# Value loads ahead of key loads in one DMA queue: an attention decode kernel that streams its cache

## The chip, the cores and the metric

The kernel runs on one core of a Trainium2 chip. The metric is device time in microseconds (us), median of several executions. All runs told of here are in the fast state. Ratios are taken against executions of the kernel before on the same chip in the same rounds. Engines are named as the profile names them: PE is TensorE (matmuls), DVE is VectorE, ACT is ScalarE, SP is SyncE, which issues nearly every load. A load is issued when SyncE hands it to the queue, and has landed when the last of its 16 semaphore events has come.

## The reference, cut to what matters

One decode step of a transformer block: 8 sequences, 32 heads, 4096 cached positions, head size 128, bf16. The parallel MLP is small.

```python
xn = layernorm(x)                                   # x: 8 x 1 x 640
q = (xn @ wq).reshape(8, 1, 32, 128).transpose(0, 2, 1, 3)
scores = einsum("bhqd,bhkd->bhqk", q, k_cache) * 128 ** -0.5
o = einsum("bhqk,bhkd->bhqd", softmax(scores), v_cache)
return x + o.reshape(8, 1, 4096) @ wo + mlp(xn)     # "@ wo" is the projection
```

The two caches are 268 MB each and every byte is used once, so the kernel is a stream of 4 MB loads with some work behind each.

## The kernel before

The caches are cut into T = 64 stretches `t`: four heads of one sequence, 4 MB of keys K(t) and 4 MB of values V(t). There are two buffers for keys and two for values. Three quarters of the key work is done on VectorE (multiply, add halves, reduce; two rounds each stretch), one quarter on TensorE (transposes and small matmuls). The softmax is done for two stretches at a time, a pair (t even, t+1). After it, PV(t), 32 matmuls of 128x512, uses V(t).

Every operation is added with a position `pos`; each engine runs its operations in the order of `pos`, and the scheduler derives the semaphore waits from the buffers named in `R` (read) and `W` (written).

```python
NK, NV, NS = 2, 2, 4                    # key buffers, value buffers
def ld(pos, dst, src, W, sem, R=()):
    add("sp", pos, lambda e: e.dma_start(dst, ...), R=R, W=W, sem=sem)
ld(-99.0, wq_sb, ...)                   # query weights, in the space of the value buffers
def pvpos(i):
    return 2.0 + i                      # PV(t) comes after the scores of t+2 on PE
for t in range(T):
    pos = (-100.0, -98.0)[t] if t < NK else t - 1.5
    ... ld(pos, K(t)) ...               # K(t+2) at t + 0.5: waits for the multiplies of t (DVE)
    pos = (0.45, 1.2)[t] if t < NV else t + 0.6
    ... ld(pos, V(t)) ...               # V(t) at t + 0.6: waits for PV(t-2) (PE)
                                        # the last V in three pieces: 64, 32, 32 columns
for hg in range(NG):
    ld(hg * B + 3.65, wo_sb, ...)       # projection weights, one load for 8 stretches
# scores of t on PE: t - 0.6 .. t - 0.1;  on DVE: t .. t + 0.13
# softmax of a pair (t, t+1): t + 1.28 .. ;  PV(t): t + 2.0 .. ;  its row sum on PE: t + 2.21
# projection on PE: 2 * pair + 5.33, behind the softmax's small matmuls of its position
```

## Time and profile before

| what | number |
|---|---|
| time, median of 3 | 1298.23 us (1298.19 to 1298.57) |
| span of the profiled run | 1296.1 us |
| read from HBM | 551.8 MB, mean 426 GB/s |
| busy: VectorE, TensorE, ScalarE | 87%, 50%, 39% |
| last value bytes landed (semaphore events of the trace) | 1290.9 us |

The page's 40 slices of the kernel before, share of the DMA engines in tenths and GB/s:

```profile
DMA  9989999999999999999999999999999999999997
GB/s 405 426 360 431 430 435 430 428 430 432 434 431 430 427 435 434 429 432 425 437 433 428 434 425 436 433 427 436 425 435 432 429 435 426 434 432 428 432 430 330
```

This is a kernel bound by its loads. Two slices fall out of line: the third (65 to 97 us) and the last.

Two stretches in the windows view of the kernel before, one around the third slice and one near the end. After the stretch and its length come the busy us of each engine with its number of instructions, the granted TensorE clock (1.00 is full), the DMA share and GB/s:

```profile
80.00:95.00 15.00, 9.48 (x112) 6.24 (x113) 14.89 (x7) 8.06 (x18) 0.00 (x0) 0.50 0.68 273
1283.00:1285.00 2.00, 1.73 (x20) 0.30 (x8) 0.00 (x0) 0.22 (x1) 0.00 (x0) 0.50 0.92 385
```

All 16 DMA engines together were silent for 2.5 us (85.74 to 88.27 in the packet records).

Issues of the loads, from the page (count, size, median us from issue to landing), and the chain of waits in its late, regular part (start, us, what):

```profile
KV_sb<-in_A_k_cache_dram SPq DMA_DIRECT2D x64, 4096.0 KB, 26.8
KV_sb<-in_A_v_cache_dram SPq DMA_DIRECT2D x63, 4096.0 KB, 35.2
```

```profile
1191.90 3.62 PE PV_ps L615 x24
1195.54 35.18 DMA KV_sb<-in_A_v_cache_dram
1230.76 3.61 PE PV_ps L615 x32
```

One value buffer is held 3.6 us by PV and in the queue for 35.2 us; with the gap, 38.86 us for a pair of stretches, 16.8 MB, 432 GB/s. A load takes 9.7 us of the queue, so a value load is asked for long before it is needed.

Who waited for whom (us in total, times, longest), engines first, then SyncE's queue:

```profile
PE PV_ps L615 <- DMA KV_sb<-in_A_v_cache_dram: 141.3, 56, 3.7
DVE Y_sb L543 <- DMA KV_sb<-in_A_k_cache_dram: 70.4, 34, 2.3
```

```profile
SPq L178 <- DVE Y_sb L543: 940.2, 56, 19.3
SPq L365 <- PE PV_ps L615: 53.7, 44, 17.8
```

SyncE waits for VectorE's multiply most of the time (940 of 1296 us), and the value load stands behind that wait in its program. Only V(3) to V(10) were issued clearly later than the end of PV(t-2), by 0.6 to 2.4 us. From V(11) on each followed PV(t-2) within about 0.2 us. K(61) and V(59) on SyncE show it, next to the chain above, where PV(57) ended at 1195.52:

```profile
1194.00 0.33 SPq L365 DMA_DIRECT2D KV_sb<-in_A_k_cache_dram  x1
1195.54 0.33 SPq L365 DMA_DIRECT2D KV_sb<-in_A_v_cache_dram  x1
```

The end, from the timeline (start, us, engine, line, operation): the last reduction on VectorE, PV(62), the three parts of PV(63), and the store of the output.

```profile
1275.31 3.35 DVE L550 TENSOR_REDUCE S_sb<-Y_sb 128x48 f32<-128x3072 bf16 x1
1281.14 3.59 PE L615 MATMUL PV_ps<-KV_sb,P_sb 128*16 128x512 bf16 x32 [1.07 <-DMA KV_sb<-in_A_v_cache_dram]
1286.03 1.04 PE L615 MATMUL PV_ps<-KV_sb,P_sb 128*16 128x512 bf16 x16
1288.51 0.80 PE L615 MATMUL PV_ps<-KV_sb,P_sb 128*16 128x512 bf16 x8 [1.45 <-DMA KV_sb<-in_A_v_cache_dram]
1290.96 1.06 PE L625 MATMUL PV_ps<-KV_sb,P_sb 128*4 128x128 bf16 x32 [0.68 <-DMA KV_sb<-in_A_v_cache_dram]
1294.36 0.35 SPq L775 DMA_DIRECT2D out_dram<-out_sb  x1
```

Each part of PV(63) starts when its piece lands, the last one 0.05 us after the last landing. 5.2 us of the span are left after it.

### The profile page before, as it was taken

The page shows a single profiled execution, that of the slowest core. Times are in us where ns is not written, and L with a number is a line of the kernel's source. Part 1 is how long each engine was busy: PE and PEld are TensorE (multiplying, and loading weights), DVE is VectorE, ACT ScalarE, POOL GpSimd, SP SyncE. Part 2 cuts the span into 40 slices and gives each one's busy share as a digit, 9 for nine tenths or more (in the row PEclk, how much of TensorE's full clock was granted, in tenths as well). Part 3 has the DMA queues.
Part 4 walks back from the last instruction along what each step waited for, and adds up shares of the span by engine and source line. Part 5 has one row for each costly group of instructions (what it writes and reads, how often), then busy time and mean ns, then how long its engine had stood idle before and what let it go on. Part 6 is the DMA issues. An engine that isn't in the chain of part 4 may idle for free.

```text
span 1296.1 us, 19692 instructions
## 1 busy us (share of the span) xinstructions
PE 650.0 (50%) x7853; PEld 408.1 (31%) x7853; DVE 1121.7 (87%) x586; ACT 500.3 (39%) x1241; POOL 0.2 (0%) x4
## 2 busy tenths in 40 slices
PE   2854554554454445454545544544544554445555
PEld 0432333333233233232333332332322332323332
DVE  3799999998898888988988988988888888889885
ACT  1543443344343243343343442443432443433442
POOL 0000000000000000000000000000000000000000
PEclk9655556555565555556555555555665556655566
DMA  9989999999999999999999999999999999999997
GB/s 405 426 360 431 430 435 430 428 430 432 434 431 430 427 435 434 429 432 425 437 433 428 434 425 436 433 427 436 425 435 432 429 435 426 434 432 428 432 430 330
DMA packets 23519, 551.99 MB, mean 426 GB/s; under 512 B 2297, under 2 KB 6481, under 8 KB 6482
## 3 DMA queue, kind: packets, MB, share of 16 engines
q1 hardware_dynamic: 23472, 551.80, 99.3%
q8 instruction: 7, 0.11, 0.0%
q14 instruction: 6, 0.05, 0.0%
q10 hardware_dynamic: 34, 0.02, 0.0%
HBM read 551.80 MB, written 0.01 MB: 426 GB/s over the span
## 4 chain that ended last, share of the span: by engine, by line
DMA 77%; DVE 10%; PE 9%; issue 3%; ACT 0%; SPq 0%; DVEq 0%
DMA KV_sb<-in_A_v_cache_dram 75%; PE PV_ps L615 7%; DVE Y_sb L543 5%; DVE Y_sb L547 3%; DVE S_sb L550 2%; DMA KV_sb<-in_A_wq_dram 2%; PE TR_ps L451 1%; PE CH_ps L564 0%; DVE M_sb L562 0%; SPq L365 0%; PE PV_ps L625 0%; PE PV_ps L689 0%; PE TR_ps L462 0%; DVE rinv_sb L596 0%; PE TR_ps L664 0%
## 5 line engine op out<-in xcount | busy, mean ns | idle before, releaser
L543 DVE TENSOR_TENSOR Y_sb<-KV_sb,qbc_sb 128x6144 bf16<-128x6144 bf16 x128 | 429.0, 3352 | 95.9 <-DMA KV_sb<-in_A_k_cache_dram 70.4
L550 DVE TENSOR_REDUCE S_sb<-Y_sb 128x48 f32<-128x3072 bf16 x128 | 429.2, 3353 | 4.4
L514 ACT ACTIVATE KT_sb<-TR_ps 128x1024 bf16<-128x1024 bf16 x256 | 254.7, 1021 | 223.4 <-PE TR_ps L511 221.9
L615 PE MATMUL PV_ps<-KV_sb,P_sb 128*16 128x512 bf16 x2040 | 224.5, 618 | 141.4 <-DMA KV_sb<-in_A_v_cache_dram 141.3
L511 PE MATMUL TR_ps<-ident_bf,KV_sb 128*128 128x128 bf16 x2048 | 249.0, 308 | 68.3 <-DMA KV_sb<-in_A_k_cache_dram 68.3
L547 DVE TENSOR_TENSOR Y_sb<-Y_sb 128x3072 bf16<-128x3072 bf16 x128 | 225.0, 1758 | 4.4
L511 PEld LDWEIGHTS TR_ps<-ident_bf,KV_sb 128*128 128x128 bf16 x2048 | 200.9, 142 | 78.7 <-DMA KV_sb<-in_A_k_cache_dram 72.8
L521 PE MATMUL S_ps<-qk_sb,KT_sb 128*128 128x4 bf16 x2048 | 98.1, 170 | 138.2 <-ACT KT_sb L514 136.5
L634 ACT ACTIVATE E_sb<-PV_ps 128x512 bf16<-128x512 f32 (+1 forms) x65 | 38.5, 592 | 318.6 <-PE PV_ps L615 316.4
L615 PEld LDWEIGHTS PV_ps<-KV_sb,P_sb 128*16 128x16 bf16 x2040 | 62.8, 124 | 253.0 <-DMA KV_sb<-in_A_v_cache_dram 146.7
L521 PEld LDWEIGHTS S_ps<-qk_sb,KT_sb 128*128 128x128 bf16 x2048 | 86.1, 109 | 169.5 <-ACT KT_sb L514 169.5
L582 ACT ACTIVATE P_sb<-S_sb,NB_sb 32x128 bf16<-32x128 f32 x256 | 101.9, 398 | 3.8
L640 PE MATMUL C_ps<-sel_bf,E_sb 128*128 128x4 bf16 x256 | 16.9, 172 | 136.6 <-DVE rinv_sb L596 113.5
L576 ACT ACTIVATE NB_sb<-CH_ps 128x2 f32<-128x2 f32 (+1 forms) x33 | 5.7, 172 | 177.2 <-PE CH_ps L572 177.2
L564 PE MATMUL CH_ps<-ident_f,M_sb 128*2 128x128 f32 (+1 forms) x33 | 12.3, 374 | 111.1 <-DVE M_sb L562 111.1
L640 PEld LDWEIGHTS C_ps<-sel_bf,E_sb 128*128 128x128 bf16 x256 | 11.4, 104 | 167.3 <-DVE rinv_sb L596 112.2
L531 ACT ACTIVATE S_sb<-S_ps 32x32 f32<-32x32 f32 x256 | 48.2, 188 | 32.1 <-PE S_ps L521 29.8
L582 ACT ACTIVATION_READ_ACCUMULATOR P_sb<-S_sb,NB_sb 32x1 f32 x256 | 47.0, 184 | 0.0
L564 PEld LDWEIGHTS CH_ps<-ident_f,M_sb 128*2 128x2 f32 (+1 forms) x33 | 2.7, 82 | 114.1 <-DVE M_sb L562 114.1
L655 DVE MEMSET oTn_sb<- 128x16 uint32 x31 | 2.2, 72 | 31.1 <-PE ACC_ps L675 31.1
L566 DVE TENSOR_REDUCE M_sb<-CH_ps 2x4 f32<-2x128 f32 (+1 forms) x33 | 9.2, 279 | 15.9 <-PE CH_ps L564 15.9
L675 PE MATMUL ACC_ps<-oTn_sb,wo_sb 128*128 128x8 bf16 x620 | 21.5, 169 | 0.0
(91 smaller groups left out, 206.1 us busy)
## 6 DMA issues: line engine op xcount, KB each, us to landing
KV_sb<-in_A_k_cache_dram SPq DMA_DIRECT2D x64, 4096.0 KB, 26.8
KV_sb<-in_A_v_cache_dram SPq DMA_DIRECT2D x63, 4096.0 KB, 35.2
KV_sb<-in_A_wq_dram SPq DMA_DIRECT2D x1, 5120.0 KB, 23.9
wo_sb<-in_A_wo_dram SPq DMA_DIRECT2D x8, 640.0 KB, 30.9
KV_sb<-in_B_w_dram SPq DMA_DIRECT2D x1, 2160.0 KB, 37.9
w_sb<-in_B_w_dram SPq DMA_DIRECT2D x1, 2080.0 KB, 43.8
KV_sb<-in_A_v_cache_dram SPq DMA_DIRECT2D x1, 2048.0 KB, 12.6
KV_sb<-in_A_v_cache_dram SPq DMA_DIRECT2D x2, 1024.0 KB, 15.1
```

The lines of the kernel that those rows point to most:

```text
L511: r = e.transpose(TR_ps[:, it.box[0], jj * P:(jj + 1) * P], kv[:, n * BK + jj, :], ident_bf[:, :])
L514: add("act", t - 0.59 + 0.12 * n, lambda e: e.activation(KT_sb[:, m % NS, :, :].rearrange("p a b -> p (a b)"), TR_ps[:, it.box[0], :], ACT ...
L521: r = e.matmul(S_ps[:, c:c + HT], KT_sb[:, m % NS, jj, :], qk_sb[:, :, i], start=True, stop=True)
L531: r = e.activation(S_sb[s, g % SR, i, 0:JP], S_ps[s, 0:JP * HT].rearrange("p (j a) -> p j a", a=HT)[:, :, a], ACT.Copy)
L543: return e.tensor_tensor(y, kv[:, j0:j1, :], qbc_sb[:, g % 2, i, :][:, None, :].to_broadcast([P, nj, P]), ALU.mult)
L547: lambda e, y=y, y2=y2: e.tensor_tensor(y2, y[:, :, 0:P // 2], y[:, :, P // 2:P], ALU.add),
L550: lambda e, y2=y2, j0=j0, j1=j1: e.tensor_reduce(S_sb[:, g % SR, i, j0:j1], y2, AX.X, ALU.add),
L582: r = e.activation(P_sb[s, i, :, a, :], S_sb[s, g % SR, i, :].rearrange("p (m c) -> p m c", c=4), ACT.Exp, bias=NB_sb[s, g % 2, i:i + 1], ...
L615: r = e.matmul(PV_ps[32 * ct:32 * ct + HT * 4, t % 2, :], P_sb[:, i, m, :, :].rearrange("p a c -> p (a c)"), vv[:, 4 * m:4 * m + 4, :].rea ...
L634: add("act", pos, lambda e: e.activation(E_sb[:, k, 0:n], PV_ps[:, k, 0:n], ACT.Copy), R=[("PV", k)] + ["wo"] * (t % GT), W=[("E", k)], X= ...
L640: r = e.matmul(OT_i, E_sb[:, t % 2, c * P:(c + 1) * P], sel_bf[:, c:HT * 4:4], start=(c == 0), stop=(c == 3 and not last))
L675: r = e.matmul(ACC_ps[:, c * B:(c + 1) * B], wo_sb[:, a, c * P:(c + 1) * P], oTn_sb[:, a, :], start=False, stop=False, skip_group_check=True)
```

## The change

The intent: SyncE should issue a value load before the key load of the same stretch of its program, so that a free value buffer is not held up by the wait for VectorE. K(63) stays ahead of V(61), since the last softmax needs it. The projection weights are issued right after a value load.

```diff
-            pos = (0.45, 1.2)[t] if t < NV else t + 0.6
+            pos = (0.45, 1.45)[t] if t < NV else t + (0.55 if t == T - 3 else 0.45)
...
-            ld(hg * B + 3.65, wo_sb[:, :, :],
+            ld(hg * B + 3.455, wo_sb[:, :, :],
```

Only SyncE's order differs: it was K(t+2), V(t), K(t+3), V(t+1) and is V(t), K(t+2), V(t+1), K(t+3).

## The prediction

> **What bounds the kernel.** HBM reads. The page moves 551.8 MB in a span of 1296.1 us; its slices show the DMA engines busy nine tenths or more nearly everywhere, at 430 to 435 GB/s. By the landings in the trace a 4 MB load lands every 9.7 us, so a pair of stretches takes 38.85 us, the period of the later chain of waits: value load 35.2 us, its PV matmuls 3.6 us, next value load. VectorE needs only 17.0 us a stretch plus 2.5 us per pair for softmax, 36.5 us. DMA is silent in two places only: 2.5 us near 86 us (a window of 10 us drops to 199 GB/s), where the queue was used up before the next key load was issued at 87.3, and the last 5 us, after the final values landed at 1290.9.
>
> **What changes.** Only the order of SyncE's queue; no byte and no other engine's order. The Trainium skill ("DMA: Bandwidth & Descriptors", Anatomy of one DMA) says that DMA engines don't wait on semaphores, the issuing sequencer does. The trace agrees: SyncE waited 940 us for the VectorE multiply that frees a key buffer. A value load is no longer behind that wait. But loads landed in the order K(t+2), V(t); afterwards V(t), K(t+2). PV(t) stands behind the scores of t+2 on TensorE, so it now waits for K(t+2) to land.
>
> **Steady state, by hand from trace durations.** Put the landing of V(t), t even, at 0. K(t+1) landed at -9.7, its reductions end at 7.3, the exponentials at about 13; K(t+2) lands at 9.7, its scores and then PV(t) end at about 22, where V(t+2) is issued. The queue still holds K(t+3) until 29.1: about 5 us of reserve after latency. The queue gets shallower (issue to landing of an even value load falls from 35 us to about 17) but doesn't run dry. No gain, no loss.
>
> **Start.** At the dry spot the first load is now V2, which waits for PV(0) to end at 89.7, not K4, free at 87.0: silence grows from 2.5 to about 5 us, +2.6 us.
>
> **End.** Key load 62 lands one load later, 39 us before the end of the reads, not 49. Two stretches on VectorE (2 x 17.0 us, softmax 1.2 us between) end 35 us later; the last exponentials end about when the last values land (8.7 us ahead of them in before). The row sum, 24 wide PV matmuls (about 2.2 us) and their eviction and extraction (1.0 us) then come after the last landing: about +3.4 us.
>
> **Prediction.** 1298.2 + 2.6 + 3.4 = 1304.2 us, range 1299.0 to 1309.0. Chances: faster by over 2% 0.01, within 2% 0.97, slower 0.02.
>
> **What would show it.** Windows 80 to 100: silence 2 to 3 us longer. Middle windows: still about 430 GB/s. Waits: PV's wait for value DMA (141 us) collapses. DMA issues: key loads longer, value loads shorter from issue to landing. Timeline at the end: VectorE's last reduction within 5 us of the last landing (12 us in before), wide PV matmuls after it.
>
> **What would make it wrong.** If PV(t) comes over 5 us later than worked out, the queue runs dry once a pair: each microsecond costs 32 us. If a shallower queue lets early DMA engines idle (one load's 16 landings spread over 1.9 us), the rate falls. If VectorE is less pressed at the end, only the start's 2.6 us remain.

## More of the kernel before

The changed kernel was timed in its own rounds only, so a difference to it by medians crosses rounds; the median of the kernel before moved by no more than 0.5 us between them (1298.06 to 1298.53).

At 80 to 95 us the queue had run dry: at 430 GB/s the 15 us would have moved 6.45 MB, 273 GB/s moved 4.10, so 5.5 us worth of bytes are missing.

## The result, and the profile after

The changed kernel takes 1306.88 us (median of 6, 1305.35 to 1307.43), the kernel before 1298.40 us (median of 6). The ratio is 1.0063, 95% interval 1.005 to 1.0076. A ratio here is the mean time of one kernel's fast runs over that of the other's of the same rounds, so not quite the ratio of the medians quoted. It is clearly slower by 0.6%, 8.5 us by the medians and 9.5 us between the two profiled runs (1297.92 and 1307.43 us, spans 1296.1 and 1305.6).

The slices and the two windows of the changed kernel:

```profile
GB/s 402 427 321 428 430 431 434 432 426 432 433 433 433 426 433 433 433 432 427 432 433 432 425 433 433 434 432 427 431 434 432 432 427 433 432 433 432 426 434 247
```

```profile
80.00:95.00 15.00, 9.09 (x102) 5.86 (x102) 14.90 (x7) 8.04 (x19) 0.00 (x0) 0.50 0.46 176
1283.00:1285.00 2.00, 2.00 (x22) 0.39 (x10) 2.00 (x1) 0.18 (x1) 0.00 (x0) 0.50 0.60 139
```

The middle is unchanged. The third slice fell from 360 to 321 GB/s: in the window of 80 to 95 us, 8.9 us worth of bytes are missing instead of 5.5 (same sum as above with 176). A second, small hole has come near 1284 us.

Issue to landing, and the chain of waits in its regular part:

```profile
KV_sb<-in_A_k_cache_dram SPq DMA_DIRECT2D x64, 4096.0 KB, 26.5
KV_sb<-in_A_v_cache_dram SPq DMA_DIRECT2D x63, 4096.0 KB, 19.1
```

```profile
1011.35 26.85 DMA KV_sb<-in_A_k_cache_dram
1038.22 3.37 DVE Y_sb L543
1041.61 1.77 DVE Y_sb L547
1043.46 3.21 issue
1046.67 3.36 DVE Y_sb L543
```

The chain now follows keys: load K(51), the two multiplies of stretch 51, then the next load. Value loads are issued only 19 us ahead of landing, key loads as far ahead as before.

The group of the PV matmuls (busy us, mean ns, then idle time of the engine before them), and the waits:

```profile
L615 PE MATMUL PV_ps<-KV_sb,P_sb 128*16 128x512 bf16 x2040 | 222.1, 613 | 0.0
DVE Y_sb L543 <- DMA KV_sb<-in_A_k_cache_dram: 81.7, 30, 4.1
```

```profile
SPq L365 <- PE PV_ps L615: 860.0, 53, 21.3
SPq L365 <- DVE Y_sb L543: 57.8, 25, 8.7
```

PV's wait of 141.3 us for values is gone: values now lie in their buffers and wait for TensorE. SyncE's long wait did not go away. It moved from VectorE's multiply to PV, since the key load now stands behind the value load's wait.

The end:

```profile
1287.20 3.35 DVE L550 TENSOR_REDUCE S_sb<-Y_sb 128x48 f32<-128x3072 bf16 x1
1291.67 0.28 PE L572 MATMUL CH_ps<-identneg,M_sb 1*32 1x1 f32 x8 [0.37 <-DVE oTn_sb L655]
1291.88 3.59 PE L615 MATMUL PV_ps<-KV_sb,P_sb 128*16 128x512 bf16 x32
1296.81 2.74 PE L615 MATMUL PV_ps<-KV_sb,P_sb 128*16 128x512 bf16 x24
1300.45 1.05 PE L625 MATMUL PV_ps<-KV_sb,P_sb 128*4 128x128 bf16 x32
1303.85 0.35 SPq L775 DMA_DIRECT2D out_dram<-out_sb  x1
```

The last value bytes landed at 1295.7 us. PV(62) had ended 0.2 us before, all of PV(63) came after it, and 9.98 us of the span were left instead of 5.23. PV(62) had begun right behind the small matmuls of the last softmax (the second line).

Landing times, read from the semaphore events of the two traces, let the 9.5 us be divided. Where the order differs, the landings are compared at which the same bytes have come in:

| point in the stream | before | after | later by |
|---|---|---|---|
| seventh 4 MB or projection load after the dry spot (V(4) before, K(6) after) | 151.2 | 154.7 | 3.5 |
| K(63) | 1261.7 | 1265.3 | 3.6 |
| last piece of V(63) | 1290.9 | 1295.7 | 4.8 |
| end of the span | 1296.1 | 1305.6 | 9.5 |

So in these two traces 3.5 us come from the dry spot at the start, 0.1 from all the stretches between, 1.2 from a hole before the last pieces, and 4.7 from work after the last landing. The first part varies from run to run: in four traces with the old order at the start (before, e1, e3, e11) the seventh load landed at 150.5 to 151.2 us, in four with the new one (the changed kernel, e2, e8, e10) at 153.2 to 154.8, on average 3.2 us later.

### The profile page after: what moved, and what is told of

Same layout as the page of the kernel before. It is cut to its first block, busy times and chain, and to the rows that moved or that the text cites. A ratio compares the mean times of both kernels' runs of the same rounds, so it can differ in the third digit from the quotient of the medians.

```text
span 1305.6 us, 19626 instructions
## 1 busy us (share of the span) xinstructions
PE 645.5 (49%) x7853; PEld 409.1 (31%) x7853; DVE 1121.6 (86%) x586; ACT 500.0 (38%) x1241; POOL 0.2 (0%) x4
## 4 chain that ended last, share of the span: by engine, by line
DMA 58%; DVE 30%; issue 8%; PE 3%; SPq 0%; ACT 0%; DVEq 0%
DMA KV_sb<-in_A_k_cache_dram 56%; DVE Y_sb L543 18%; DVE Y_sb L547 7%; DVE S_sb L550 5%; DMA KV_sb<-in_A_wq_dram 2%; PE TR_ps L451 1%; PE PV_ps L615 0%; SPq L365 0%; PE ACC_ps L675 0%; PE CH_ps L564 0%; DVE M_sb L562 0%; DVE M_sb L566 0%; PE CH_ps L572 0%; ACT E_sb L634 0%; PE PV_ps L625 0%
## 6 DMA issues: line engine op xcount, KB each, us to landing
KV_sb<-in_A_k_cache_dram SPq DMA_DIRECT2D x64, 4096.0 KB, 26.5
wo_sb<-in_A_wo_dram SPq DMA_DIRECT2D x8, 640.0 KB, 11.6
```

## The experiments

Theory A: the loss sits at the two ends, as the table says. Theory B, the rival: the queue is shallower and every pair loses a little, 8.5 us over 32 pairs. All outputs are right.

| run | edit | median us (range) | before, same rounds | ratio, 95% interval |
|---|---|---|---|---|
| e1_start_undone | V(2) behind K(4) again | 1301.91 (1301.71 to 1303.84) | 1298.53 | 1.0032 (1.0018 to 1.0046) |
| e2_end_undone | V(60) behind K(62) again | 1305.83 (1303.46 to 1307.48) | 1298.53 | 1.0059 (1.0045 to 1.0072) |
| e3_both_undone | both | 1303.04 (1300.86 to 1303.88) | 1298.53 | 1.0035 (1.0021 to 1.0048) |
| e8_after_no_exception | V(61) ahead of K(63) | 1306.21 (1304.97 to 1306.77) | 1298.53 | 1.0057 (1.0043 to 1.0071) |
| e4_before_wq_first | before, query weights first | 1293.10 (1292.95 to 1293.63) | 1298.06 | 0.9961 (0.9948 to 0.9975) |
| e5_after_wq_first | changed, query weights first | 1298.18 (1296.34 to 1298.69) | 1298.06 | 0.9994 (0.998 to 1.0008) |
| e6_before_slow_pv | before, 88 extra matmuls a pair | 1298.57 (2 runs) | 1298.06 | 1.0003 (0.9985 to 1.0021) |
| e7_after_slow_pv | changed, 88 extra | 1325.49 (2 runs) | 1298.06 | 1.021 (1.0192 to 1.0229) |
| e10_last14_undone | last 14 stretches as before | 1304.20 (1303.53 to 1305.51) | 1298.34 | 1.0047 (1.0033 to 1.0061) |
| e11_start_last14_undone | that and V(2) behind K(4) | 1301.28 (1300.76 to 1302.00) | 1298.34 | 1.0022 (1.0008 to 1.0035) |
| e12_after_slow_pv2 | changed, 176 extra | 1382.87 (2 runs) | 1298.34 | 1.065 (1.0631 to 1.0669) |
| e13_before_slow_pv2 | before, 176 extra | 1377.09 (2 runs) | 1298.34 | 1.0606 (1.0586 to 1.0625) |

### The start alone: e1_start_undone

```diff
-t + (0.55 if t == T - 3 else 0.45)
+t + (0.6 if t == 2 else 0.55 if t == T - 3 else 0.45)
```

> The changed kernel, with value load 2 alone put back behind key load 4. Theory A (the loss sits at the two ends: about 3 us at the dry queue near 86 us, about 6 us in the last 40 us, nothing between): the silence of the DMA engines near 86 us goes back from 5.5 to about 2.5 us and the time falls by 3 to 3.5 us, from 1306.9 to about 1303.5; the end stays as late after the last landing (about 10 us, before 5). Theory B (every pair of stretches loses a little, 8.5 us over 32 pairs, since the queue is shallower): at most 0.3 us comes back, 1306.6 or more.

Measured: 1301.91 us, 5.0 us less than the changed kernel by medians and 0.0031 by the ratios, 4.0 us. The silence of the DMA engines is back at 2.5 us (85.41 to 87.95), the seventh load after it lands at 151.2 us and K(63) at 1261.7, both as in the kernel before. So the start costs 3.5 us of landing time and the middle nothing. Theory B is out. (The hole before the last pieces stays: they land 1.4 us later than in the kernel before.) The time fell somewhat more than 3.5 us. The extra is at the end, where the same 24 matmuls of PV(63) took 1.47 us instead of 2.74. The windows view shows why; the tail of the changed kernel, then that of this one:

```profile
1296.00:1303.00 7.00, 5.43 (x83) 2.71 (x83) 0.38 (x2) 0.99 (x3) 0.00 (x0) 0.50 0.01 2
```

```profile
1292.00:1297.00 5.00, 3.03 (x75) 1.76 (x79) 0.38 (x2) 1.40 (x3) 0.00 (x0) 1.00 0.01 3
```

The granted TensorE clock was 0.50 in one tail and 1.00 in the other. Three groups of matmuls in the tail (the 24, the 32 small ones at L625, the last 16 at L664) took 4.5 us in the one and 2.6 in the other: 1.9 us between two kernels whose last loads and matmuls stand in the same order. The Trainium skill ("TensorE: Matmul & The Clock Gate", Part 1: The HAM clock gate) says that the clock is decided in free-running windows of 3413 ns. The clock records of these traces agree: the stretches of one granted clock are nearly all whole multiples of 3.413 us. The changed kernel's times are spread over 2.1 us and those of the kernel before over 1.3. That the clock's phase in the tail makes this difference is a guess and not shown: there is one trace for each kernel, and e10, whose tail is as short as that of the kernel before, is spread over 2.0 us.

### The end, too little undone: e2_end_undone and e3_both_undone

```diff
-t + (0.55 if t == T - 3 else 0.45)
+t + (0.6 if t == T - 4 else 0.55 if t == T - 3 else 0.45)          # e2
+t + (0.6 if t in (2, T - 4) else 0.55 if t == T - 3 else 0.45)     # e3
```

> The changed kernel, with value load 60 alone put back behind key load 62. Theory A: the last key work is again 49 us ahead of the end of the reads, the wide PV matmuls of stretch 63 run as their pieces land, the out store follows the last landing by about 5 us instead of 10, and the pause of the queue before the last value pieces (about 1 us) goes; the time falls by 5.5 to 6 us to about 1301. Theory B: at most 0.3 us comes back.

> Both: values 2 and 60 behind their keys again, all loads from value 3 to value 59 still ahead of theirs. Theory A: the time of the kernel before, 1298.4 within 0.7 us, though 57 of 64 stretches have the new order; middle windows at 428 to 435 GB/s. Theory B: about 1306.

Measured: e2 gave back only about 1 us by medians (its own times are spread over 4 us), e3 came to 1303.04 us instead of 1298.4. My design was wrong, and the traces say where. In e3 the landings run 0.7 us ahead of those in the kernel before from the seventh load on (150.5 us) and are still 0.7 us ahead at K(63) (1261.0): with V(2) and V(60) moved back, 57 reordered values cost the stream nothing. That part of theory A holds, and theory B is refuted a second time. That the last bytes then land at 1290.8 us, as in the kernel before (1290.9), is chance: the early lead made up for 0.6 us of a hole before the last pieces, which moving V(60) back did not remove. But the tail after the landing is still 8.3 us, not 5.2. K(62) does land one load earlier, and it is of no use. VectorE in e2:

```profile
1249.16 3.35 DVE L550 TENSOR_REDUCE S_sb<-Y_sb 128x48 f32<-128x3072 bf16 x1
1253.44 0.28 DVE L566 TENSOR_REDUCE M_sb<-CH_ps 2x4 f32<-2x128 f32 x1 [0.47 <-PE CH_ps L564]
1254.94 3.35 DVE L543 TENSOR_TENSOR Y_sb<-KV_sb,qbc_sb 128x6144 bf16<-128x6144 bf16 x1
```

K(62) had landed at 1245.2 us, but VectorE finished stretch 61 at 1252.5 and started 62 at 1254.9, because K(61) was late too. VectorE needs 36.5 of the 38.86 us of a pair, so it idles 2.4 us a pair and needs four or five pairs to get one load (9.7 us) ahead.

### The exception for K(63): e8_after_no_exception

```diff
-t + (0.55 if t == T - 3 else 0.45)
+t + 0.45
```

> The changed kernel without its exception: value load 61 too goes ahead of key load 63, which then lands one load (9.7 us) later. Theory A: VectorE could not start stretch 63 before 1273.6 us anyway, and key 63 would land near 1275.0, so only about 1.5 us are lost: about 1308.4. If instead the landing of key 63 itself sets the end, the loss is near 9.7 us: about 1316. Theory B says nothing.

Measured: 1306.21 us, 0.7 us less than the changed kernel, where 1.5 more were expected. VectorE did start stretch 63 1.5 us later (1275.07 against 1273.59), and PV(62) started 1.5 us later too (1293.39 against 1291.88), as expected:

```profile
1293.39 3.59 PE L615 MATMUL PV_ps<-KV_sb,P_sb 128*16 128x512 bf16 x32
1298.10 1.47 PE L615 MATMUL PV_ps<-KV_sb,P_sb 128*16 128x512 bf16 x24
```

In this run's tail the granted clock was 0.91, and the three groups of matmuls took 2.6 us, not 4.5, which more than hides it. K(63) landed at 1275.05 us and VectorE began 0.02 us later, so here the landing was the limit. Of the 9.7 us that it came later, VectorE's own lag swallowed 8.3. In the traced runs the exception is worth 1.5 us of the chain; by the times of all executions it can't be told from nothing.

### The dry spot removed: e4_before_wq_first and e5_after_wq_first

```diff
-            pos = (-100.0, -98.0)[t] if t < NK else t - 1.5
+            pos = (-98.5, -98.0)[t] if t < NK else t - 1.5      # K(0) after the query weights
```

> The kernel before, with the query weights loaded ahead of key 0 rather than behind it. They land near 15 us instead of 25, so the query projection and VectorE's first stretch start about 10 us earlier; key load 4 is then issued near 77 us, before the queue runs dry at 85.7. Theory A (that silence of 2.5 us delays everything after it by as much): the silence near 86 us is gone and the time falls by 2.5 us to about 1296. If the time lost there is made up later: no change.

> The same move in the changed kernel. Theory A: PV(0) ends near 80 us instead of 90, value load 2 is issued before the queue is dry, the silence of 5.5 us goes and the time falls by about 5.5 us to about 1301.4; the late end stays. Theory B: at most a few tenths.

Measured: 1293.10 and 1298.18 us, 5.0 us less than the kernel before and 8.7 less than the changed one. The last landing came 4.9 and 8.1 us earlier; the rest of the 8.7 is in the tail, which varies. The hole is gone in both; the window of 80 to 95 us of e4, then of e5:

```profile
80.00:95.00 15.00, 8.83 (x126) 5.80 (x118) 12.66 (x7) 6.20 (x12) 0.00 (x0) 0.69 1.02 437
```

```profile
80.00:95.00 15.00, 10.16 (x122) 6.45 (x118) 13.06 (x7) 5.71 (x11) 0.00 (x0) 0.50 1.03 439
```

Two things follow. First, nothing lost in the dry spot is made up later. Second, both gains are larger than I expected (2.5 and 5.5) and are near the missing bytes instead (5.5 and 8.9 us). They are nearer still to the idle share of the DMA engines in the windows of 80 to 95 us: 0.32 and 0.54 of 15 us are 4.8 and 8.1 us. I had taken the time in which all DMA engines were silent for the cost. The Trainium skill ("DMA: Bandwidth & Descriptors", Why a DMA increments its semaphore by 16 and not by 1) says that the up to 16 engines of one DMA finish independently. The traces agree: the 16 landings of K(3), the last load before the silence, are spread over 1.8 us, so the queue runs dry engine by engine before all are silent. After a silence, a load took 12.2 us from issue to landing (K(4) in before) where the stream has one every 9.7.

With the dry spot out of both kernels, the changed order is slower by 5.1 us (1298.18 against 1293.10), which is nearly all the cost of the end: of the 5.6 us between the two traces, 0.5 arise before K(63) has landed, 1.0 before the last pieces and 4.1 after the last landing. And e4 beats both kernels of the case: it is 0.4% faster than the kernel before in the same rounds (interval 0.25 to 0.52%), which is itself faster than the changed one.

### The reserve: e6, e7, e12 and e13

```diff
+                def pe_pv(e, q=q, extra=22 if q == 0 and t % 2 == 0 and 0 < t < T - 2 else 0):
+                    for ct in list(range(4)) * extra:          # results thrown away
+                        e.matmul(PV_ps[...], P_sb[...], vv[...], start=True, stop=True)
```

(e12 and e13: `extra=44`.)

> The kernel before with 88 extra PV matmuls (a repeated first group, its result thrown away, about 10 us) ahead of PV(t) for even t from 2 to 60. This tests the reserve: in before a value load is issued about 35 us ahead of its landing, its own transfer takes 9.7 and latency 2 to 3, so some 22 us of reserve; 10 us more cost nothing in the middle: within 2 us of 1298.4.

> The same 10 us of extra matmuls in the changed kernel. The even value loads are issued 17 us ahead of landing; a load into an empty queue takes 12.3 us from issue to landing (value load 2), so the reserve is about 5 us and 10 us more run the queue dry once a pair: 4 to 5.5 us for each of 30 pairs, 120 to 165 us, about 1430 to 1470. If the order of the two loads made no difference to the reserve: within 2 us of 1307.

Measured: the kernel before doesn't notice (1298.57 us); the changed kernel loses 18.6 us (each new kernel ran twice). That is the direction expected and far less than the 120 us expected. The extra matmuls run dense, 72 ns each, and the PV behind them takes 1.9 us and not 3.6, so the end of PV(t) moved by 4.4 us and not by 10 (from 21.7 to 26.1 us after the landing of V(t); V(12) in the changed kernel, V(28) in e7). That is nearly all of the reserve of about 5 us, and the delay varies: even value buffers are held for 24.0 to 27.6 us in e7, where they were held for 21.4 to 21.9. In 12 of 29 pairs the landings fall back, mostly by 1 to 3 us. Two windows of e7 next to each other, the second with such a hole:

```profile
640.00:650.00 10.00, 8.90 (x132) 4.97 (x136) 9.90 (x5) 4.03 (x8) 0.00 (x0) 0.65 1.01 436
650.00:660.00 10.00, 6.64 (x110) 4.69 (x102) 7.74 (x4) 4.34 (x7) 0.00 (x0) 0.86 0.94 383
```

So the order does cost reserve in the middle, though no time as long as nothing uses the reserve. To see the cliff itself I doubled the extra work.

> The 88 extra matmuls delayed the end of PV(t) by about 4.4 us net only (they run dense at 72 ns, and the PV behind them in 1.9 us, not 3.6) and cost 18 us in all: just the 5 us of reserve. Now 176 in the changed kernel: a net delay of about 11 us, 6 more than the reserve; about 5 to 6 us for each of 30 pairs, 1460 to 1500. If the reserve were larger than I think and the 18 us came from something else, for example the extra work itself: about 1345.

> The same 176 extra matmuls in the kernel before, whose reserve is about 22 us: no cost, within 2 us of 1298.4.

Measured: 1382.87 and 1377.09 us. Both expectations failed, and the pair of runs doesn't measure the reserve. In e13, the kernel before with more extra work, another loop closes: VectorE takes its instructions in order and one of them, the reciprocal of the row sum, stands behind PV(t) on TensorE.

```profile
DVE rinv_sb L596 <- PE C_ps L593: 156.1, 31, 6.0
```

In the kernel before that wait was 6.0 us in all. Here it is 156.1 (101.1 in e12), and VectorE falls behind. That the time is then set by VectorE, softmax, scores and PV in turn, in both orders, is my reading of these waits; no run tests it. How large the reserve of the kernel before is beyond 4.4 us stays open.

### The end, undone over 14 stretches: e10_last14_undone and e11_start_last14_undone

```diff
-t + (0.55 if t == T - 3 else 0.45)
+t + (0.6 if t >= T - 14 else 0.45)                # e11: t == 2 or t >= T - 14
-            ld(hg * B + 3.455, wo_sb[:, :, :],
+            ld(hg * B + (3.65 if hg == NG - 1 else 3.455), wo_sb[:, :, :],
```

> Undoing value load 60 alone gave back only 1 us, and the trace shows why: key load 62 landed 10 us earlier, but VectorE was still busy with stretch 61, whose key was as late as in the changed kernel; VectorE idles only some 2.4 us a pair, so it needs four or five pairs to work off one load. So now the changed kernel with the order of before for the last 14 stretches (values 50 to 63 and the last projection weights behind their keys). Theory A: the whole cost of the end, about 5 us, comes back, 1301.5 to 1302; VectorE's last reduction ends some 12 us ahead of the last landing, and the output store follows the last landing by about 4 us, as in before; the start stays dry for 5.5 us. Rival C (the late end has another cause than late keys on VectorE): no more than the 1 us of the single swap comes back, 1305.5 to 1306.

> The last run with value load 2 behind key load 4 as well, so that values 3 to 49 alone have the new order. Theory A (no loss in the middle): the time of before, 1298.4 within 0.7 us. If the middle loses even 0.1 us a pair, over 1300.

Measured: 1304.20 and 1301.28 us, about 3 us more than expected in both. The tail is settled: 5.2 us in both from the last landing to the end of the span, as in the kernel before, and VectorE's last reduction ends 13 us ahead of the last landing. So late keys on VectorE make the late tail; rival C is out. The missing 3 us are a fault of the experiment. In e11 the landing of K(51) at 1034.6 equals that of V(49) in the kernel before, the same bytes; then the queue runs dry. SyncE in e11 from there:

```profile
1027.52 0.42 SPq L365 DMA_DIRECT2D KV_sb<-in_A_v_cache_dram  x1
1053.90 0.38 SPq L365 DMA_DIRECT2D wo_sb<-in_A_wo_dram  x1
1054.33 0.51 SPq L365 DMA_DIRECT2D KV_sb<-in_A_k_cache_dram  x1
1054.87 0.43 SPq L365 DMA_DIRECT2D KV_sb<-in_A_v_cache_dram  x1
```

I had moved only the last load of projection weights back. The one before it stood, in the seam between the two orders, ahead of K(53), and waited for a projection that ends after the softmax of stretches 50 and 51, at 1053.9. K(53) had been free since 1046.4 (the end of the multiplies of stretch 51). In both kernels the landings fall back by 2.3 us there. They lose another 1.3 us by the last landing (1294.5 in e11, 1290.9 in before), 1.1 of it in e11 between K(63) and V(61). Reckoned by the first of each load's 16 semaphore events, e11 stays 4.0 us behind the kernel before from the seam to the end. Only the last events fall back at K(63) (the spread of a load's events grows from 0.7 to 1.7 us); why is not known. A wait at the head of an in-order queue is paid by whatever stands behind it.

## Why the prediction was right, and where it was off

It said 1304.2 us, +6.0, range 1299 to 1309; measured were 1306.9 us, +8.5. It said "within 2%" with 0.97, and so it was.

- **"No gain, no loss" in the steady state: right.** From 154.7 us to K(63) the landings keep the distance of 3.5 us to about 0.2. The kernel was bound by its loads, and the order of a full queue doesn't change how fast it drains. The wait it removed (940 us of SyncE behind VectorE) was off the critical path, and from V(11) on it had not even held a value load.
- **Start, +2.6 us: right in mechanism, a little small.** V(2) waits for PV(0), as said; 3.5 us were lost in the traced run and 3.2 on average over the traces. Of the difference in the traced run, 0.7 us is that PV(0) ended at 90.4 us in it, not 89.7. The term also took the silence for the cost: 5.5 us of silence, 3.0 more than before.
- **End, +3.4 us: right that late keys make the tail late, wrong in the wait between, mis-sized.** 4.7 us (profiled run). The term reckoned only PV(63) after the last exponentials. It overlooked that PV(62) too stands behind the last softmax's small matmuls in TensorE's order: PV(62) started at 1291.9 us, right after them, and PV(63) at 1296.8. The exponentials had ended at 1294.2 us, 1.4 before the last landing, and were not what PV(63) waited for. From the last landing it took 1.15 us until PV(63) began, 2.74 for its 24 matmuls at the low granted clock (reckoned as 2.2; 1.47 in e1 and e8 at the higher clock) and 0.90 for eviction and extraction.
- **A term that was missing: 1.2 us.** The first piece of V(63) waits for PV(61), PV(61) for the scores of 63, and those on ScalarE for the exponentials of 62, which are late because VectorE is. The piece was issued at 1283.1 us, 1.6 us before V(62) had landed: too late to follow without a hole (139 GB/s at 1283 to 1285 us). All terms that were off were too small, so no errors cancelled.
- **"Key loads longer": wrong.** They stayed at 26.5 us (26.8 before). In a stream with a fixed period, issue to landing is the period less the time the buffer is held: 38.86 - 12.1 = 26.8 us for keys before and 38.86 - 12.6 = 26.3 now (medians from landing to the next issue into the buffer), 38.86 - 3.6 = 35 us for values before. For even values it is 38.86 - 21.7 = 17 now, as predicted. The order lengthened mainly how long a value buffer is held.
- The predicted marks otherwise came: PV's wait for values went from 141.3 us to 0.0, VectorE's last reduction ended 5.1 us before the last landing (12.3 before).

What stays open: the projection weights' new place was not tried alone. In e3 it is in force, and the landings keep a constant lead of 0.7 us over the kernel before, so it cost the stream nothing there.

## What to carry to other kernels

Before removing a long wait, look whether it delays anything: here the value loads behind it had to wait for PV anyway. When a kernel is bound by one in-order load queue that never runs dry, reordering the queue need not change any time in the middle, as here; look at the places where it does run dry, and at what the last loads have to feed. Put in front what the longest chain behind the loads needs, and read the reserve of each buffer as period less holding time. Count a dry spot in missing bytes or in the idle share of the DMA engines, not in common silence, and remove it with something that can be loaded or started earlier: here, loading the query weights before the first keys was worth more than any order of the stream that was tried.

## What the Trainium skill lacked or had wrong

- "DMA: Bandwidth & Descriptors", Bandwidth: it gives 425 GB/s for a 16 MB transfer on one core, and says in one place that about 358 GB/s binds loads from HBM, in another that this is each core's share when both cores of the HBM domain stream. Here, with this program on one core, loads of 4 MB in a row held 429 to 434 GB/s over windows of 100 us, so the second reading fits. What two cores get, no run here shows.
- No page says what a dry queue costs. Here 2.5 us in which all DMA engines were silent cost 4.9 us of landing time (e4 against before), 5.5 us of silence cost 8.1 (e5 against the changed kernel).
- "DMA: Bandwidth & Descriptors", Anatomy of one DMA: its fit for gpsimd-issued loads, 2.0 us plus bytes over 436 GB/s, gives 11.6 us for 4 MB (an estimate from that page). A SyncE-issued load into an empty queue took 12.2 to 12.3 us.
- "TensorE: Matmul & The Clock Gate", Part 1: The HAM clock gate, tells of the clock in matmul streams and in bursts between waits for DMA. It does not treat a short tail of matmuls on the critical path, where the same three groups took 4.5 or 2.6 us here.
